# Retention and MLP on one core: a ring of ten turned chunks, one operation per state sum, step waits on the unit ahead, and new places for turns and steps

## The chip, the cores and the metric

The kernel runs on one core of a Trainium2 chip. The metric is device time in microseconds (us) of one execution, the median of several runs. A core has TensorE (PE, matmuls; its weight loads are shown as PEld), VectorE (DVE), ScalarE (ACT), GpSimd (POOL) and SyncE (SP), each with a queue that runs in order, and DMA engines that all queues share.

## The reference

Eight heads of causal retention (attention without softmax, with a decay per head) over eight sequences of 576 tokens, then an MLP with a sigmoid GELU over all 4608 tokens:

```python
scores = scale * np.matmul(q, k.transpose(0, 1, 3, 2))          # q, k, v: 8 x 8 x 576 x 64
gamma = 1.0 - 2.0 ** (-5.0 - np.arange(H, dtype=np.float32))
Dmat = np.where(rel >= 0, gamma[:, None, None] ** rel[None, :, :], 0.0)
attn_out = np.matmul(scores * Dmat[None, :, :, :], v)
x = attn_out.transpose(0, 2, 1, 3).reshape(B * S, H * D)         # 4608 x 512
h = x @ w_in                                                     # w_in: 512 x 2048
out = (h * (1.0 / (1.0 + np.exp(-1.702 * h)))) @ w_out           # w_out: 2048 x 512
```

## The kernel before, in words

**MLP.** The 4608 tokens are nine chunks of 512. For a chunk c, `hidden(c, f)` (L670) makes 128 hidden columns: four matmuls of 512 columns into a PSUM bank (psH[0], psH[1], and psU where it rotates over three), then a GELU on ACT that frees the bank. `hidden_half` (L705) does two f for half a chunk, eight matmuls of 256 columns. `project(c, r, g)` (L727) adds four of sixteen f for the row block r of 128 tokens; after g = 3 the bank is copied to one of three buffers osb (by DVE, or by ACT in chunk 0) and stored by SP. Each of these is a unit of four large matmuls (or eight half ones). From chunk 3 on, `region(c)` mixes the sixteen hidden units of chunk c with the sixteen projections of chunk c - 1, which all use psU.

**Retention.** A batch is five chunks of up to 128 tokens (chunk number n = 5 b + c) or nine blocks of 64. The decay is split into factors on v (`scale_v`, L344, on DVE) and on the output (gq); so a block needs masked scores within the block and a state, the running sum of k-transposed times v, across blocks. Batch 0 is done by chunks; batches 1 to 7 in 21 steps of three blocks, m = 0 to 20. `burst(m_out, m_in)` (L524) runs on PE some 90 matmuls of 64 x 64 x 64 back to back: values and state parts of the outputs of step m_out, and states and scores of step m_in = m_out + 1. Behind it DVE evacuates m_out to xT (`evac_wide`, which the MLP reads), masks the scores of m_in (`mask_wide`), adds the states up over the blocks into zacc (`state_wide`, L637) and casts them to zw, which the next burst reads. The state parts lie in columns 384 to 511 of PSUM banks 1 to 3 and in bank 4 (`z_at`, L520), which the transposes on PE also use.

**Loads and turns.** POOL's queue loads q, k and v chunk by chunk with a cast to bf16 into a ring of three batches; `step(m)` (L866) issues the loads of batch b + 3 into the freed places. The scores need q and k turned (head dimension on partitions). `turn(n)` does it on PE with a copy by ACT (chunks 4 to 9), `turn_dma(n)` (L481) with two DMA transposes on SP's queue, into a ring `qk` of NQK = 6 buffers; `step(m)` issues them six chunks ahead, so a turn waits until the slot's old chunk has been read. Stores of the output are on SP's queue too.

**The order.** It is written out by hand: `run(units, between)` (L880) calls the units in turn, and `between` names what is put behind unit i: turns, scalings, bursts, steps. `Rec` (L43) records each operation with what it reads and writes, derives the waits on semaphores, and leaves out a wait that an earlier one on the same queue covers. An operation's waits stand right before its first instruction, so what a burst needs is waited for inside the burst, part by part.

Of the kernel before, what the change touches and what calls it, by code (L numbers as in the profile page):

```python
# [27 lines left out]
NQK = 6  # L28
# [103 lines left out]
def bass_retnet_parallel__then__act_gelu_quick_kernel(  # L132
# [11 lines left out]
    with es:  # L144
# [373 lines left out]
        z_low = {0: (1, 384), 1: (3, 384), 2: (2, 384)}  # L518

        def z_at(blk, r):  # L520
            return z_low[blk] if r else (4, 128 * blk)


        def burst(m_out, m_in):  # L524
# [32 lines left out]
            def state(e, blk, first=()):  # L557
                g = blocks(m_in)[blk]
                for t in range(2):
                    for j in range(2):  # L560
                        for u in range(2):
                            h = 4 * u + 2 * t + j
                            bank, off = z_at(blk, place(g, u)[1])
# [6 lines left out]
            def score(e):  # L570
                for blk, g in enumerate(blocks(m_in)):
                    for t in range(2):
                        for u in range(2):
# [3 lines left out]
                            for j in range(2):  # L577
# [3 lines left out]
                                             start=(x == 0 and j == 0), stop=True,  # L581
# [12 lines left out]
            if m_in is not None:  # L594
                b, cs = chunks(m_in)
                rs = [(nm, b % NST, c) for nm in "kv" for c in cs]
                rq = [("qk", (NC * b + c) % NQK, 1) for c in cs] + queries(m_in)

                def state_a(e):
                    state(e, 1, (3, 4) if fresh else (4,))  # L600
                    return state(e, 0, (1,))
                before = R.op("PE", state_a, r=rs, ps=["S", "Z", "W"])
                R.op("PE", score, r=rq, ps=["S"])
                if m_in % 3 < 2:
                    R.op("PE", lambda e: state(e, 2, (2,) if fresh else ()), r=rs,
                         ps=["O", "W"], own=None if fresh else before)
                    done = None
                else:
                    done = done and before
# [6 lines left out]
            if m_in is not None:  # L616
                mask_wide(m_in)
                state_wide(m_in)
# [18 lines left out]
        def state_wide(m):  # L637
            keys = ["S", "W", "Z", "O"]

            def add(src, blk, lo, hi, first):  # L640
                to, was = zacc[:, blk, lo:hi], zacc[:, (blk - 1) % 3, lo:hi]
                if hi - lo == 256:
                    to, was = (x.rearrange("p (u x) -> p u x", u=2) for x in (to, was))
                if first:
                    R.op("DVE", lambda e: e.tensor_copy(to, src), w=[("zacc", blk)], ps=keys)
                else:
                    R.op("DVE", lambda e: e.tensor_tensor(to, was, src, ALU.add),  # L647
                         r=[("zacc", (blk - 1) % 3)], w=[("zacc", blk)], ps=keys)

# [347 lines left out]
```

## Time and profile before

| | |
|---|---|
| median of 3 runs | 319.37 us (316.39 to 320.68) |
| profiled execution | 318.88 us, of which 316.6 us are the span from the first to the last instruction |
| mean granted clock of TensorE over the span | 0.984 of full |
| DMA packets | 154848, of which 145472 under 512 bytes |

How to read it: the page gives busy shares of each engine and a picture of the span in 40 slices of 7.9 us. A row of the waits names the engine, the tile and line of the operation that waited, what released it, and the sum, the number and the longest of the waits in us. A row of the timeline gives start and length in us, engine, line, operation, output and inputs with shapes, how many, and in brackets the idle time before it with what ended it. A row of windows gives a stretch, then busy time of PE, PEld, DVE, ACT and POOL, the granted clock, the DMA share and GB/s. Ends of matmuls are modelled, and a few of their records are missing.

### The profile page before, as it was taken

To read this page: it belongs to the slowest core of one execution; us is meant where nothing else is said; L and a number is where in the kernel's file an instruction comes from. 1 tells how busy PE (TensorE), PEld (TensorE's weight loads), DVE (VectorE), ACT (ScalarE), POOL (GpSimd) and SP (SyncE) were. 2 spreads that over 40 slices of the span, in tenths; PEclk is the share of its full clock that TensorE was granted. 3 is DMA by queue.
4 is the path that set the end of the run, shared out by engine and by line. 5 is a ranking of instruction groups with operands and counts; after the bars stand their busy time and mean duration, and the time that the engine had idled before them with its cause. 6 is when DMAs were issued, how large, how long until landed. Compare 5 with 4: busy or idle time off the path is not lost.

```text
span 316.6 us, 7664 instructions
## 1 busy us (share of the span) xinstructions
PE 292.9 (93%) x3358; PEld 149.1 (47%) x3395; DVE 148.8 (47%) x274; ACT 108.3 (34%) x182; POOL 155.5 (49%) x208
## 2 busy tenths in 40 slices
PE   7799995979977977999999999999999999999996
PEld 3454443856733433444444444444444444444444
DVE  6699716066583775663462066606660420011011
ACT  8676240621403441333333332333233333333300
POOL 8999999999999999999610000000000000000000
PEclk9999998799997999999999999999999999999999
DMA  9999999999999999999999134313300000000102
GB/s 74 152 194 193 176 164 222 157 154 119 159 157 173 168 133 148 146 190 144 188 160 148 68 58 88 97 55 68 93 35 33 35 35 33 33 33 35 66 35 98
DMA packets 154848, 35.76 MB, mean 113 GB/s; under 512 B 145472, under 2 KB 150336, under 8 KB 154816
## 3 DMA queue, kind: packets, MB, share of 16 engines
q0 software_dynamic: 118384, 18.36, 83.3%
q1 hardware_dynamic: 36432, 16.92, 27.7%
q8 instruction: 26, 0.43, 0.5%
q14 instruction: 6, 0.05, 0.1%
HBM read 36.70 MB, written 9.44 MB: 146 GB/s over the span
## 4 chain that ended last, share of the span: by engine, by line
PE 76%; DVE 11%; DMA 5%; POOL 4%; issue 3%; POOLq 0%
PE psU L730 28%; PE psH L677 27%; PE psH L730 6%; DMA w_out_sb<-in_moe_w_out_dram 4%; PE psH L714 3%; DVE zacc L647 3%; PE psA L536 2%; PE psA L578 2%; DVE sm L634 2%; DVE xT L623 2%; PE psU L714 2%; DMA st_k<-in_k_dram 2%; PE psA L564 1%; POOL st_q L208 1%; PE psA L552 1%
## 5 line engine op out<-in xcount | busy, mean ns | idle before, releaser
L682 ACT ACTIVATE gT<-psH 128x512 bf16<-128x512 f32 x116 | 69.3, 597 | 147.4 <-PE psH L677 147.4
L677 PE MATMUL psH<-xT,w_in_sb 128*128 128x512 bf16 x453 | 110.3, 383 | 3.7 <-DVE osb L742 2.1
L730 PE MATMUL psU<-w_out_sb,gT 128*128 128x512 bf16 x416 | 100.9, 379 | 2.3 <-issue 2.2
L221 POOL DMA_DIRECT2D st_k<-in_k_dram x70 | 75.3, 1425 | 1.0 <-DVE st_v L291 1.0
L221 POOL DMA_DIRECT2D st_v<-in_v_dram x70 | 73.7, 1382 | 2.5 <-PE psA L552 2.5
L677 PEld LDWEIGHTS psH<-xT,w_in_sb 128*128 128x128 bf16 x464 | 43.5, 98 | 60.2 <-ACT gT L682 7.3
L730 PEld LDWEIGHTS psU<-w_out_sb,gT 128*128 128x128 bf16 x432 | 41.1, 98 | 47.8
L208 POOL DMA_DIRECT2D st_q<-in_q_dram x40 | 58.1, 1453 | 0.2 <-issue 0.2
L742 DVE COPY osb<-psU 128x512 f32<-128x512 f32 x26 | 17.9, 688 | 72.4 <-PE psU L730 72.4
L623 DVE TENSOR_TENSOR xT<-psA,gq 128x768 bf16<-128x768 f32 x21 | 20.1, 958 | 52.9 <-PE psA L552 52.9
L730 PE MATMUL psH<-w_out_sb,gT 128*128 128x512 bf16 x120 | 28.7, 379 | 1.4 <-issue 0.8
L634 DVE TENSOR_TENSOR sm<-psA,maskw 128x768 bf16<-128x768 f32 x21 | 19.9, 949 | 16.7 <-PE psA L564 16.7
L647 DVE TENSOR_TENSOR zacc<-zacc,psA 128x128 f32<-128x128 f32 (+1 forms) x77 | 24.8, 322 | 2.2
L350 DVE TENSOR_TENSOR st_v<-st_v,vfac 128x512 bf16<-128x512 bf16 x37 | 24.2, 681 | 3.4 <-DMA st_v<-in_v_dram 3.4
L730 PEld LDWEIGHTS psH<-w_out_sb,gT 128*128 128x128 bf16 x128 | 11.9, 98 | 14.0 <-DMA w_out_sb<-in_moe_w_out_dram 0.9
L536 PE MATMUL psA<-sm,st_v 64*64 64x64 bf16 x504 | 11.9, 197 | 3.0 <-DVE zw L663 2.8
L371 ACT ACTIVATE qk<-psA 128x1024 bf16<-128x1024 bf16 x10 | 10.2, 1023 | 11.7 <-PE psA L365 11.7
L714 PE MATMUL psH<-xT,w_in_sb 128*128 128x256 bf16 x88 | 12.8, 298 | 1.1 <-DVE xT L623 1.1
L536 PEld LDWEIGHTS psA<-sm,st_v 64*64 64x64 bf16 x504 | 7.6, 107 | 12.4 <-issue 6.8
L720 ACT ACTIVATE gT<-psH 128x512 bf16<-128x512 f32 x11 | 6.6, 598 | 18.7 <-PE psH L714 18.7
L663 DVE CAST zw<-zacc 128x768 bf16<-128x768 f32 (+1 forms) x21 | 11.6, 550 | 0.7
L564 PE MATMUL psA<-st_v,st_k 64*64 64x64 bf16 x448 | 9.9, 195 | 1.4 <-DVE st_v L350 1.4
(99 smaller groups left out, 199.9 us busy)
## 6 DMA issues: line engine op xcount, KB each, us to landing
out_dram<-osb SPq DMA_DIRECT2D x35, 256.0 KB, 2.0
st_q<-in_q_dram POOLq DMA_DIRECT2D x32, 128.0 KB, 11.3
st_k<-in_k_dram POOLq DMA_DIRECT2D x57, 64.0 KB, 11.6
st_v<-in_v_dram POOLq DMA_DIRECT2D x57, 64.0 KB, 12.2
w_out_sb<-in_moe_w_out_dram POOLq DMA_DIRECT2D x4, 512.0 KB, 11.1
w_in_sb<-in_moe_w_in_dram POOLq DMA_DIRECT2D x3, 512.0 KB, 8.4
st_k<-in_k_dram POOLq DMA_DIRECT2D x4, 128.0 KB, 4.2
st_v<-in_v_dram POOLq DMA_DIRECT2D x4, 128.0 KB, 4.8
```

The source lines that it names most:

```text
L208: R.op("POOL", lambda e, d=d, s=s: e.dma_start(d, s), w=[(nm, sl, c)], dma=(nm, sl, c))
L221: R.op("POOL", lambda e: [e.dma_start(d, s) for d, s in parts], w=[(nm, sl, c)], dma=(nm, sl, c), parts=2)
L350: R.op(eng, lambda e: e.tensor_tensor(t, t, f, ALU.mult), r=[("vfac", min(b, 1))], w=[("v", sl, c)])
L536: i = e.matmul(psA[half(t), 2 + u, at : at + 64], rows_of(st_v, m_out, g, u, 4 * u + 2 * t + j), smw[si(m_out)][half(r), j, 2 * blk + t, : ...
L623: R.op("DVE", lambda e: e.tensor_tensor(xT[:, :, t0 : t0 + 192].rearrange("p (u j) n -> p u j n", u=2), psA[:, 2:4, 0:384].rearrange("p u ...
L634: R.op("DVE", lambda e: e.tensor_tensor(o, i, k, ALU.mult), r=["maskw"], w=[("sm", si(m))], ps=["S"])
L647: R.op("DVE", lambda e: e.tensor_tensor(to, was, src, ALU.add), r=[("zacc", (blk - 1) % 3)], w=[("zacc", blk)], ps=keys)
L677: i = e.matmul(bank.ap(), w_in_sb[:, a, 128 * f : 128 * f + 128], xT[:, a, 512 * c : 512 * c + 512], start=(a == 0), stop=(a == 3))
L682: R.op("ACT", lambda e: e.activation(gT[c % 2][:, f, :], bank.ap(), AF.Gelu_apprx_sigmoid), w=[("gT", c % 2, f)], ps=[key])
L714: m = e.matmul(bank[:, 256 * i : 256 * i + 256], w_in_sb[:, a, 128 * (f + i) : 128 * (f + i) + 128], xT[:, a, a0 : a0 + 256], start=(a == ...
L730: i = e.matmul(bank, gT[c % 2][:, f, 128 * r : 128 * r + 128], w_out_sb[:, f, :], start=(f == 0), stop=(f == NF - 1))
L742: R.op("DVE", lambda e: e.tensor_copy(osb[m].ap(), bank), w=[("osb", m)], ps=[key])
```

## The change

- `NQK` 6 to 10: ten buffers for turned chunks. `step(m)` now issues the turns of the chunks of step m + 5 (`turn_step`), before its loads; steps 3 and 4 are turned ahead of step 0.
- `z_at` is keyed by step, block and half u in place of the row half r, so that the two parts of one state always lie as one access pattern with two segments: `state_wide` adds each block with one operation of 2 x 128 columns; it took two of 128 for each block of odd number.
- PE's order within a burst: state of block 1, scores, then the states of blocks 0 and 2 as one operation.
- `needs(m_out, m_in)` lists all that a burst reads. `run` gives that list as `ahead` to the unit in front of a `step`, which waits for it before its first matmul. Bursts that aren't in a `step`, and `hidden_half`, don't do so.
- The first burst comes one unit earlier, adds its states before the mask and has them cast by ACT.
- Step 2 also takes in step 3 (its states and scores were a burst of their own, four half units into the second half of chunk 1). Other places move by a unit or so; chunk 2's hidden units begin on psH[1] in place of psH[0].

The diff, cut to its core:

```diff
-NQK = 6
+NQK = 10
...
-        z_low = {0: (1, 384), 1: (3, 384), 2: (2, 384)}
-
-        def z_at(blk, r):
-            return z_low[blk] if r else (4, 128 * blk)
-
-
-        def burst(m_out, m_in):
+        def z_at(m, blk, u):
+            if u == 0:
+                return 4, 128 * blk
+            odd = blocks(m)[blk] % 2
+            return (3 if odd else 2) if blk == 2 else 1 - odd, 384
+
+
+        def needs(m_out, m_in):
+            r = []
+            if m_out is not None:
+                b, cs = chunks(m_out)
+                r += [("sm", si(m_out)), "zw"] + [("v", b % NST, c) for c in cs] + queries(m_out)
+            if m_in is not None:
+                b, cs = chunks(m_in)
+                r += [(nm, b % NST, c) for nm in "kv" for c in cs]
+                r += [("qk", (NC * b + c) % NQK, 1) for c in cs] + queries(m_in)
+            return r
+
+        def burst(m_out, m_in, cast="DVE"):
...
-                    state(e, 1, (3, 4) if fresh else (4,))
-                    return state(e, 0, (1,))
-                before = R.op("PE", state_a, r=rs, ps=["S", "Z", "W"])
-                R.op("PE", score, r=rq, ps=["S"])
-                if m_in % 3 < 2:
-                    R.op("PE", lambda e: state(e, 2, (2,) if fresh else ()), r=rs,
-                         ps=["O", "W"], own=None if fresh else before)
-                    done = None
-                else:
-                    done = done and before
+                opened = z_at(m_in, 1, 1)[0]
+                done = R.op("PE", lambda e: state(e, 1, (opened, 4)), r=rs, ps=["S", "W"])
+                R.op("PE", lambda e: score(e, (1 - opened,)), r=rq, ps=["S"])
+
+                def state_b(e):
+                    i = state(e, 0)
+                    if m_in % 3 < 2:
+                        i = state(e, 2, (2, 3) if fresh else ())
...
                 R.op("PE", phase_y, r=ro, ps=["O", "Z"], own=done)
                 evac_wide(m_out)
-            if m_in is not None:
+            if m_in is not None and cast == "ACT":
+                state_wide(m_in, cast)
                 mask_wide(m_in)
-                state_wide(m_in)
+            elif m_in is not None:
+                mask_wide(m_in)
...
-        def state_wide(m):
-            keys = ["S", "W", "Z", "O"]
-
-            def add(src, blk, lo, hi, first):
-                to, was = zacc[:, blk, lo:hi], zacc[:, (blk - 1) % 3, lo:hi]
-                if hi - lo == 256:
-                    to, was = (x.rearrange("p (u x) -> p u x", u=2) for x in (to, was))
-                if first:
-                    R.op("DVE", lambda e: e.tensor_copy(to, src), w=[("zacc", blk)], ps=keys)
-                else:
-                    R.op("DVE", lambda e: e.tensor_tensor(to, was, src, ALU.add),
-                         r=[("zacc", (blk - 1) % 3)], w=[("zacc", blk)], ps=keys)
-
+        def state_wide(m, cast):
             flat = psA.ap().rearrange("p a n -> p (a n)")
             gs = [g for g in blocks(m) if g < NBLK - 1]
             for blk, g in enumerate(gs):
-                (b1, o1), (b0, o0) = z_at(blk, 1), z_at(blk, 0)
-                at1, at0 = 512 * b1 + o1, 512 * b0 + o0
-                if g % 2 == 0:
-                    src = flat[:, at1 : at1 + 128]
-                    src = bass.AP(src.tensor, src.offset, [src.ap[0], [at0 - at1, 2], [1, 128]])
-                    add(src, blk, 0, 256, g == 0)
+                at1, at0 = (512 * x + y for x, y in (z_at(m, blk, 1), z_at(m, blk, 0)))
+                src = flat[:, at1 : at1 + 128]
+                src = bass.AP(src.tensor, src.offset, [src.ap[0], [at0 - at1, 2], [1, 128]])
+                to, was = (zacc[:, x % 3, :].rearrange("p (u x) -> p u x", u=2)
+                           for x in (blk, blk - 1))
+                if g == 0:
+                    R.op("DVE", lambda e, to=to, src=src: e.tensor_copy(to, src),
+                         w=[("zacc", blk)], ps=["S", "W", "Z", "O"])
                 else:
-                    add(flat[:, at0 : at0 + 128], blk, 0, 128, False)
-                    add(flat[:, at1 : at1 + 128], blk, 128, 256, False)
+                    R.op("DVE", lambda e, to=to, src=src, was=was: e.tensor_tensor(
+                        to, was, src, ALU.add),
+                        r=[("zacc", (blk - 1) % 3)], w=[("zacc", blk)], ps=["S", "W", "Z", "O"])
             z = zw[:, gs[0] + 1 : gs[0] + 1 + len(gs)].rearrange("p b u t d -> p b (u t d)")
-            R.op("DVE", lambda e: e.tensor_copy(z, zacc[:, 0 : len(gs), :]),
-                 r=[("zacc", x) for x in range(len(gs))], w=["zw"])
+            r = [("zacc", x) for x in range(len(gs))]
+            if cast == "ACT":
+                R.op("ACT", lambda e: e.activation(z, zacc[:, 0 : len(gs), :], AF.Copy), r=r, w=["zw"])
+            else:
+                R.op("DVE", lambda e: e.tensor_copy(z, zacc[:, 0 : len(gs), :]), r=r, w=["zw"])
...
+        def hidden(c, f, rotate=2, ahead=()):
...
+            R.op("PE", fn, r=[("w_in", f // 2)] + [("xT", x) for x in toks] + list(ahead), ps=[key])
...
         def step(m, into=True):
             b, i = 1 + m // 3, m % 3
             burst(m, m + 1 if into and m + 1 < NWIDE else None)
+            turn_step(m + 5)
             for c in ((0,), (1, 2), (3, 4))[i]:
-                n = NC * b + c + NQK
-                if PE_TURNS <= n < NSTEP:
-                    turn_dma(n)
                 if b + NST < B:
                     load(b + NST, c)
+        def step_chunks(m):
+            return [NC * (1 + m // 3) + c for c in ((0, 1), (2, 3), (4,))[m % 3]] if m < NWIDE else []
+
+        def turn_step(m):
+            for n in step_chunks(m):
+                turn_dma(n)
+
         def scale(m):
-            for c in ((0, 1), (2, 3), (4,))[m % 3]:
-                scale_v(NC * (1 + m // 3) + c)
+            for n in step_chunks(m):
+                scale_v(n)
         def run(units, between):
             for i, unit in enumerate(units):
-                unit()
+                ahead = []
+                for fn, *args in between.get(i, ()):
+                    if fn is step:
+                        ahead += needs(args[0], args[0] + 1 if len(args) < 2
+                                       and args[0] + 1 < NWIDE else None)
+                unit(ahead)
                 for fn, *args in between.get(i, ()):
                     fn(*args)
         def unit_h(c, half, f):
-            return lambda: hidden_half(c, half, f)
+            return lambda ahead: hidden_half(c, half, f)
         def unit_o(c, r, g, bank, eng="DVE"):
-            return lambda: project(c, r, g, *bank, eng=eng)
+            return lambda ahead: project(c, r, g, *bank, eng=eng, ahead=ahead)
         run([unit_o(0, r, g, wide_banks[(1, 2, 0)[r]], "ACT") for g in range(4) for r in range(3)]
             + [unit_o(0, 3, g, wide_banks[1], "ACT") for g in range(4)],
             {1: [(tail_turn,)], 3: [(intra, 4)], 5: [(tail_out,)], 6: [(turn, 5)],
-             8: [(scale_v, 5)], 12: [(turn, 6), (scale_v, 6)], 14: [(burst, None, 0)]})
+             8: [(scale_v, 5)], 11: [(turn, 6), (scale_v, 6)], 13: [(burst, None, 0, "ACT")]})
+        turn_step(3)
+        turn_step(4)
         step(0, False)
-        turn_dma(10)
         hcount[0] = 16
         run([unit_h(1, 0, f) for f in range(0, NF, 2)],
             {0: [(turn, 7), (scale_v, 7)], 2: [(turn, 8), (scale_v, 8)],
-             5: [(burst, None, 1)], 6: [(turn, 9), (scale_v, 9)]})
+             4: [(turn, 9), (scale_v, 9)], 6: [(burst, None, 1)]})
         run([unit_o(1, r, g, wide_banks[(1, 2)[r]]) for r in range(2) for g in range(4)],
-            {0: [(step, 1)], 4: [(step, 2, False)], 5: [(scale, 3)]})
+            {0: [(scale, 3)], 1: [(step, 1)], 5: [(step, 2)]})
         run([unit_h(1, 1, f) for f in range(0, NF, 2)],
-            {3: [(burst, None, 3)], 5: [(scale, 4)]})
+            {3: [(scale, 4)]})
         run([unit_o(1, r, g, wide_banks[(0, 1)[r - 2]]) for r in range(2, 4) for g in range(4)],
-            {1: [(step, 3)], 3: [(scale, 5)], 5: [(step, 4)]})
-        hcount[0] = 0
-        run([lambda f=f: hidden(2, f, 3) for f in range(NF)],
-            {1: [(scale, 6)], 3: [(step, 5)], 5: [(scale, 7)], 8: [(step, 6)],
-             10: [(scale, 8)], 13: [(step, 7)]})
+            {0: [(step, 3)], 2: [(scale, 5)], 4: [(step, 4)]})
+        hcount[0] = 1
+        run([lambda ahead, f=f: hidden(2, f, 3, ahead) for f in range(NF)],
+            {0: [(scale, 6)], 2: [(step, 5)], 5: [(scale, 7)], 7: [(step, 6)],
+             10: [(scale, 8)], 12: [(step, 7)]})
```

20 lines of the change are left out of this document (10 added, 10 removed).

## The prediction

> **What bounds the kernel now.** I read the page first, for the shares and the slices of the span.
>
> ```profile
> span 316.6 us, 7664 instructions
> ...
> PE 292.9 (93%) x3358; PEld 149.1 (47%) x3395; DVE 148.8 (47%) x274; ACT 108.3 (34%) x182; POOL 155.5 (49%) x208
> ...
> PE   7799995979977977999999999999999999999996
> ...
> DMA  9999999999999999999999134313300000000102
> ```
>
> TensorE is the bound, but its slices show two halves: from the sixteenth slice on it is full, and between slices 6 and 16 (about 42 to 125 us) it is not, while the DMA engines are. Nearly all that placing can win lies in that stretch. Next the waits of PE, in total us, times and longest:
>
> ```profile
> PE psA L536 <- DVE zw L663: 2.8, 2, 2.2
> PE psA L578 <- issue: 2.5, 2, 1.8
> PE psH L677 <- DVE osb L742: 2.1, 1, 2.1
> PE psA L365 <- DVE zacc L647: 1.6, 1, 1.6
> PE psA L564 <- DVE st_v L350: 1.4, 3, 0.8
> ...
> PE psH L714 <- DVE xT L623: 1.1, 1, 1.1
> ...
> PE psH L677 <- DVE zacc L647: 0.8, 1, 0.8
> ```
>
> Except for the second row they are all waits for VectorE, and none is for a turned chunk: the ring of six cost TensorE nothing here. The 0.8 is region 3's first hidden unit on bank psH[0], which the last unit of chunk 2 (15 mod 3 = 0) used just before; ACT's GELU is what it waits for, whatever the label says. Third the stretches by window, for the granted clock (the number behind those of the five engines, 1.00 being full):
>
> ```profile
> 93.78:97.19 3.41, 1.27 (x7) 0.42 (x6) 3.31 (x8) 0.00 (x0) 3.41 (x6) 1.00 1.79 142
> 97.19:100.60 3.41, 3.41 (x10) 1.22 (x9) 0.86 (x2) 0.90 (x2) 3.41 (x7) 0.50 1.64 186
> 121.08:124.49 3.41, 1.48 (x44) 0.94 (x38) 1.08 (x2) 0.00 (x0) 3.41 (x6) 1.00 1.74 138
> ```
> ```profile
> 53.78:62.85 9.07, 9.07 (x64) 7.06 (x64) 1.14 (x2) 4.82 (x7) 9.07 (x14) 0.68 2.12 167
> ```
>
> After a stretch of 3.41 us with 1.27 us of PE work the clock is halved (0.50 in the next row); a stretch with 1.48 did not halve it. So the two long waits cost twice: behind the 2.2 us one 9.07 x (1 - 0.68) = 2.9 us, behind the 2.1 us one 3.41 x 0.50 = 1.7 us. Together 4.6 us.
>
> **The pieces for the sum.** PE first, then VectorE behind a step (one step of the steady half), then the forms.
>
> ```profile
> 126.91 2.59 PE psH L677 x12
> ```
> ```profile
> 198.00 1.03 PE L730 MATMUL psU<-w_out_sb,gT 128*128 128x512 bf16 x4
> 198.96 0.32 PE L536 MATMUL psA<-sm,st_v 64*64 64x64 bf16 x16
> 199.11 0.23 PE L552 MATMUL psA<-qk,zw 64*64 64x64 bf16 x8
> ...
> 200.10 0.81 PE L730 MATMUL psU<-w_out_sb,gT 128*128 128x512 bf16 x3 [0.16 <-issue]
> ```
> ```profile
> 192.09 0.96 DVE L623 TENSOR_TENSOR xT<-psA,gq 128x768 bf16<-128x768 f32 x1 [2.66 <-PE psA L552]
> 192.96 0.94 DVE L634 TENSOR_TENSOR sm<-psA,maskw 128x768 bf16<-128x768 f32 x1
> 193.82 0.41 DVE L645 COPY zacc<-psA 128x256 f32<-128x256 f32 x1
> 194.27 1.06 DVE L647 TENSOR_TENSOR zacc<-zacc,psA 128x128 f32<-128x128 f32 x3
> 195.37 0.56 DVE L663 CAST zw<-zacc 128x768 bf16<-128x768 f32 x1
> 195.84 0.68 DVE L742 COPY osb<-psU 128x512 f32<-128x512 f32 x1
> 196.45 1.28 DVE L350 TENSOR_TENSOR st_v<-st_v,vfac 128x512 bf16<-128x512 bf16 x2
> ```
> ```profile
> L647 DVE TENSOR_TENSOR zacc<-zacc,psA 128x128 f32<-128x128 f32 x56 | 16.0, 286 | 1.7
> ...
> L647 DVE TENSOR_TENSOR zacc<-zacc,psA 128x256 f32<-128x256 f32 x21 | 8.8, 417 | 0.5
> L663 DVE CAST zw<-zacc 128x512 bf16<-128x512 f32 x7 | 3.0, 429 | 0.2
> ```
>
> A matmul of 512 columns takes 2.59 / 12 = 0.216 us, a unit of four 0.86. A full step takes about 1.0 us: from 198.96 to 200.10, less 0.216, since of the next unit only three of four records are there. So the unit behind this step began at about 199.88.
>
> *State sums.* A block of two 128-column parts took two operations of 286 ns when its number is odd and one of 417 ns when even; now always one. Four blocks of eight in each batch change: 4 x (572 - 417) = 0.6 us of VectorE per batch, 28 operations less in all. VectorE is 47% busy, so this counts only where its chain ends a wait. The bounds for the new operation are 417 (same pattern of two parts) and 572; I take 417, which starts every 0.45 us.
> The chain behind a step, counted from the start of the next unit: evacuation begins at 0.12, takes 0.87, mask 0.87, three sums 1.35, cast 0.56: 3.77 us; with two sums and the short cast, when a batch ends, 0.12 + 0.87 + 0.87 + 0.90 + 0.43 = 3.19. An output copy adds 0.61, a scaling of one chunk 0.65, of two 1.28.
>
> *Waits on the unit ahead.* The unit before a step now waits for all that the step needs. What stands behind it on PE is the whole program, so the cover of VectorE's chain is one unit (0.86) shorter at each step. In the regions from chunk 3 on, seven units remain: 7 x 0.86 = 6.04 against 3.77 + 0.61 + 1.28 = 5.66 us. No wait there, by 0.4 us. In the crowded stretch the cover is shorter, and each place has a new wait (chain, then cover):
> - step 1: behind a burst without outputs there is no evacuation: 3.77 - 0.87 = 2.9, plus 0.05 to reach PE, less 2 units: 1.2
> - step 2: 3.19 + 0.05 - 3 units = 0.65
> - second unit of the second half of chunk 1, on psH[1]: step 2 now carries the next batch's scores and sums, and row block 1's output copy queues behind them: 3.77 + 0.68 + 0.05 - 3 units = 1.9
> - step 4: 3.77 + 0.65 + 0.05 - 3 units = 1.9
> - step 5: 3.19 + 0.68 + 1.28 + 0.05 - 5 units = 0.9
> - step 6: 3.77 + 1.28 + 0.05 - 4 units = 1.65
> - step 7: 3.77 + 0.65 + 0.05 - 4 units = 1.0
> - step 8: 3.19 + 1.28 + 0.05 - 4 units = 1.1
>
> What the waits give back is at the steps themselves. The first small matmul came 0.31 us after the last large one (198.00 + 3 x 0.216 to 198.96), 0.095 more than the cadence; and where the scores of a new batch wait for turned chunks there is a hole:
>
> ```profile
> 102.39 0.30 PE L564 MATMUL psA<-st_v,st_k 64*64 64x64 bf16 x16
> 102.68 0.38 PE L578 MATMUL psA<-qk 64*64 64x64 bf16 x24
> ```
>
> Sixteen take 0.15 (198.96 to 199.11), so 0.14 us is lost there, at seven of some twenty steps. Per step the gain is between 0 and 0.095 + 0.14 = 0.23; I take 0.11, as the lead may belong to the change of tile shape: 20 x 0.11 = 2.2 us. The waits themselves, once met, are taken at nothing ahead of a unit, since 0.86 us of large matmuls of the unit before run meanwhile; were that cover gone, 0.14 each would come back.
>
> *First burst.* It moves one unit ahead (two units now cover it, not one), its sums go before the mask, and its cast to ACT. ACT's price is not in the trace for this form; the nearest rows are
>
> ```profile
> L682 ACT ACTIVATE gT<-psH 128x512 bf16<-128x512 f32 x116 | 69.3, 597 | 147.4 <-PE psH L677 147.4
> ...
> L371 ACT ACTIVATE qk<-psA 128x1024 bf16<-128x1024 bf16 x10 | 10.2, 1023 | 11.7 <-PE psA L365 11.7
> ```
>
> so 0.60 to 1.02, midway 0.81, beside the mask's 0.95 and hidden by it (if ACT took more than 0.95, the rest would lie on the path). Chain: 0.12 + 1.35 + 0.95 + 0.05 = 2.47, less 1.73 = 0.75, in place of 2.2. The 1.1 for xT behind it stays. Idle there falls to 0.75 + 1.0, so 1.65 us of a 3.41 us stretch is work, above the 1.48 that kept the clock: I count the 2.9 us as gone.
> *Turn 9 before burst 1*: the 1.6 for the bank of the turns goes; late next is step 1, above. *Bank order of chunk 2* (starts on psH[1]): the 2.1, its 1.7 of half clock and the 0.8 go; late next are steps 5 and 8. *Step 2 merged with burst 3*: one restart of about 0.2 less.
> *Ring of ten.* Turns no longer wait for a free slot but for the loads:
>
> ```profile
> SPq L484 <- PE psA L552: 29.3, 12, 6.8
> ```
> ```profile
> 93.50 2.22 POOL L221 DMA_DIRECT2D st_k<-in_k_dram  x2
> ```
> ```profile
> st_k<-in_k_dram POOLq DMA_DIRECT2D x2, 64.0 KB, 13.2
> qk<-st_q SPq DMA_TRANSPOSE x1, 7.3
> ```
>
> Direct gain 0, as TensorE never waited for them. They pass the output stores on SP: each store now stands behind the turns of five steps ahead, and those behind their loads. The tightest is chunk 23 (its load of k is the row at 93.50): it lands at about 107.5 (94.2 for its second half + 13.2), and is ready at about 117, 2 us of SP's queue and 7.3 from issue later. Step 8 ended at about 123.3 (row 122.90 below); 7 us earlier, and with seven units behind it, step 9 wants chunk 23 at about 122. POOL's own queue keeps its order.
>
> **The sum**, against the profiled execution (318.88 us, span 316.6), which is 0.15% under the median of the runs, 319.37. Gone or replaced: the waits 2.8 + 2.1 + 1.6 + 1.4 + 0.8 = 8.7. They are eight, and each is about 0.18 longer from start to start than the profile's idle, which counts from the modelled end of a matmul (sixteen show 0.32 where 0.15 pass): + 1.4 = 10.1. Clock 4.6, merged burst 0.2, and the mid-operation stalls 2.5 + 0.36 = 2.9. Total 17.8. New: 0.75 + 1.2 + 0.65 + 1.9 + 1.9 + 0.9 + 1.65 + 1.0 + 1.1 = 11.05, and half of the mid-operation stalls, 1.45 (below): 12.5. 17.8 - 12.5 + 2.2 = 7.5; from this I take 0.6 for loads that the earlier turns delay (the late-turns rival below costs 3 and I count a fifth of it): 6.9. Time 318.9 - 6.9 = 312.0.
>
> The mid-operation stalls fall inside one operation, where no wait can be, beside one instruction packet (DMA view of 119 to 120.5 us):
>
> ```profile
> 122.90 0.22 PE L578 MATMUL psA<-qk 64*64 64x64 bf16 x4 [1.77 <-issue]
> ```
> ```profile
> q8 instruction: 1, 0.02, 4.9%
> ```
>
> The bounds after the change are 0 and 2.9, since where a block of instructions ends moves: half. [...]
>
> **Rivals.**
> - *The new waits halve the clock.* Two are 1.9 us and leave 3.41 - 1.9 = 1.51 us of work in a stretch, the line lies between 1.27 and 1.48; step 0's place is as near. One such costs 1.7, two 3.4: 313.7 to 315.4. For: nearness, and stretches can begin elsewhere. Against: each alone lies on the good side. [...]
> - *Turns late.* Two or three more chunks are turned by 110 us than before, on full DMA engines. If chunk 23 comes 7 us later, step 9 waits 2 us, and a store behind the turns can hold an output copy for 1 more: 315.
> - *Slower.* The shorter cover fails in the regions: if the chain takes 7.2 us in place of 5.66 (two-part sums at 572, copies waiting for stores), each of twelve steps waits 1.2: 14 us, 326. It decides from 0.6 a step (chain 6.6) on. Against it: the steady rows above end at 197.73, 5.85 behind their unit, before the saving.
> - *No stalls in mid-operation, step gain at 0.2*: 309.
>
> **How the numbers follow.** Chances: forecast 0.53 (310.5 to 313.5), last rival 0.12, half clock 0.15, late turns 0.12, slower 0.08. The range 308.5 to 316.5 holds all but the last and the tails. About 2% (6.4 us, 313.0 from the median) is what a measurement here can tell from no change: faster 0.60 (most of the forecast and the last rival), same 0.32, slower 0.08.
>
> **What would show it.** Right: clock 1.00 from 50 to 100 us; a wait of about 1.9 before the second unit of the second half of chunk 1, labelled osb; PE waits on zw or st_v now before large units (L730, L677) instead of L536 and L564; no hole ahead of the scores; step 0's wait under 1 us. Wrong: waits on turned chunks or on stores, a half clock behind the 1.9 us waits, or waits before the regions' steps.

## The result and the profile after

The changed kernel takes 315.25 us (median of 18 runs, 313.65 to 316.96) against 318.12 (18 runs, 316.39 to 320.68) beside it: a ratio of 0.9901, interval 0.9872 to 0.9929. The gain is clear of the noise, about 2.9 us, and under the 2% line. The profiled execution took 316.69 us (span 314.8); that of before 318.88 (316.6).

The page's span, busy shares, PE's slices, the granted clock and the DMA slices of the kernel after:

```profile
span 314.8 us, 7671 instructions
...
PE 296.1 (94%) x3395; PEld 148.7 (47%) x3395; DVE 144.2 (46%) x245; ACT 109.0 (35%) x183; POOL 155.0 (49%) x208
...
PE   7899987977979788999999999999999999999996
...
PEclk9999999899899999999999999999999999999999
DMA  9999999999999999999999995100000000000112
```

The picture is the old one: a stretch up to about 125 us in which TensorE is not full, then full slices. The DMA engines are full far beyond it, to about 189 us here (24 slices of 7.87 us) and 174 us before. Two slices still show a lowered clock. The waits of PE (total us, times, longest):

```profile
PE psH L722 <- DVE osb L750: 2.0, 1, 2.0
...
PE psU L685 <- DVE st_v L350: 1.7, 1, 1.7
PE psH L738 <- DVE st_v L350: 1.7, 1, 1.7
PE psH L738 <- DVE zw L672: 1.6, 2, 1.1
PE psH L685 <- DVE st_v L350: 1.4, 2, 0.9
...
PE psH L722 <- DVE xT L637: 1.1, 1, 1.1
PE psH L738 <- DMA w_out_sb<-in_moe_w_out_dram: 0.8, 1, 0.8
PE psU L738 <- DVE st_v L350: 0.7, 1, 0.7
PE psA L576 <- issue: 0.7, 1, 0.7
PE psA L548 <- ACT zw L670: 0.6, 1, 0.6
```

As the prediction said, the waits now stand ahead of large units (L685, L738, L722) and no longer inside bursts, apart from step 0's (the last row). They are not shorter: the waits for VectorE and ScalarE shown here sum to 10.8 us; those of the prediction's list, from before, sum to 9.8. The stretches around the two places with a lowered clock (us, busy time of PE, PEld, DVE, ACT and POOL, granted clock, DMA share, GB/s):

```profile
50.20:53.61 3.41, 1.68 (x51) 1.37 (x51) 2.42 (x4) 1.07 (x2) 3.41 (x6) 1.00 1.81 238
53.61:57.02 3.41, 3.41 (x22) 2.66 (x21) 0.80 (x2) 2.22 (x3) 3.41 (x5) 0.50 2.10 198
74.09:77.50 3.41, 1.40 (x12) 0.92 (x11) 3.31 (x7) 0.60 (x1) 3.41 (x6) 1.00 2.53 137
77.50:80.92 3.42, 3.42 (x18) 2.44 (x17) 0.99 (x2) 0.65 (x2) 3.42 (x7) 0.50 1.37 121
```

In this execution the clock is halved behind step 0's two short waits, and again behind the 2.0 us wait for the output copy: half of 3.41 us, 1.7, at each place.

One profile says little about the clock here, though. Each run lists its mean granted clock, and it comes in steps of about 0.0054 (0.995, 0.989, 0.984 and 0.978 in the runs), which is one stretch of 3.41 us at half clock (3.41 x 0.5 / 315). Of 69 runs of the kernel before, taken beside the experiments, none had full clock throughout; their mean is 0.9896, or 1.9 such stretches. 26 runs with one stretch have a median of 316.9 us, 25 with two 317.8, 16 with three 318.5 (the other two have four): about 0.8 us a stretch. Of the 18 runs of the kernel after, 12 had full clock (median 314.5), four one stretch (316.0), two had two (316.8, the profiled one among them): mean 0.9976, or 0.44 stretches. So about 1.5 stretches fewer at 0.8 to 1.2 us each, 1.2 to 1.8 us of the 2.9, are clock. This is an estimate from differences between runs; the clock alone does not tell the time of a variant, as experiments 2 and 9 show.

### The profile page after: what moved, and what is told of

Same layout as the page of the kernel before. It is cut to its first block, busy times and chain, and to the rows that moved or that the text cites. A ratio compares the mean times of both kernels' runs of the same rounds, so it can differ in the third digit from the quotient of the medians.

```text
span 314.8 us, 7671 instructions
## 1 busy us (share of the span) xinstructions
PE 296.1 (94%) x3395; PEld 148.7 (47%) x3395; DVE 144.2 (46%) x245; ACT 109.0 (35%) x183; POOL 155.0 (49%) x208
## 4 chain that ended last, share of the span: by engine, by line
PE 77%; DVE 14%; DMA 4%; POOL 2%; issue 2%; ACT 1%; POOLq 0%
PE psU L738 28%; PE psH L685 27%; PE psH L738 4%; DMA w_out_sb<-in_moe_w_out_dram 4%; PE psH L722 3%; DVE zacc L664 3%; DVE xT L637 2%; PE psA L548 2%; DVE sm L648 2%; PE psH L799 2%; PE psA L576 2%; PE psU L722 2%; DVE st_v L350 2%; PE psA L365 1%; PE psA L590 1%
## 5 line engine op out<-in xcount | busy, mean ns | idle before, releaser
L685 PE MATMUL psH<-xT,w_in_sb 128*128 128x512 bf16 x464 | 110.2, 379 | 1.4 <-DVE st_v L350 1.4
L738 PE MATMUL psU<-w_out_sb,gT 128*128 128x512 bf16 x432 | 104.5, 379 | 0.7 <-DVE st_v L350 0.7
L685 PEld LDWEIGHTS psH<-xT,w_in_sb 128*128 128x128 bf16 x464 | 43.1, 98 | 58.1 <-ACT gT L690 7.3
L221 POOL DMA_DIRECT2D st_k<-in_k_dram x70 | 65.6, 1140 | 4.6 <-issue 3.6
L221 POOL DMA_DIRECT2D st_v<-in_v_dram x70 | 65.1, 1139 | 0.0
L738 PEld LDWEIGHTS psU<-w_out_sb,gT 128*128 128x128 bf16 x432 | 41.0, 98 | 48.8 <-DVE st_v L350 1.4
L208 POOL DMA_DIRECT2D st_q<-in_q_dram x40 | 48.4, 1209 | 5.8 <-issue 5.8
L738 PE MATMUL psH<-w_out_sb,gT 128*128 128x512 bf16 x128 | 30.3, 380 | 4.1 <-DVE st_v L350 1.7
L664 DVE TENSOR_TENSOR zacc<-zacc,psA 128x256 f32<-128x256 f32 x49 | 20.5, 418 | 1.2
L738 PEld LDWEIGHTS psH<-w_out_sb,gT 128*128 128x128 bf16 x128 | 11.6, 98 | 18.4 <-DVE zw L672 2.6
L722 PE MATMUL psH<-xT,w_in_sb 128*128 128x256 bf16 x88 | 12.3, 294 | 3.1 <-DVE osb L750 2.0
L576 PE MATMUL psA<-st_v,st_k 64*64 64x64 bf16 x448 | 11.6, 197 | 0.7 <-issue 0.7
L685 PE MATMUL psU<-xT,w_in_sb 128*128 128x512 bf16 x40 | 10.3, 380 | 1.8 <-DVE st_v L350 1.7
```

Of the source, the lines that this page charges most:

```text
L208: R.op("POOL", lambda e, d=d, s=s: e.dma_start(d, s), w=[(nm, sl, c)], dma=(nm, sl, c))
L221: R.op("POOL", lambda e: [e.dma_start(d, s) for d, s in parts], w=[(nm, sl, c)], dma=(nm, sl, c), parts=2)
L664: R.op("DVE", lambda e, to=to, src=src, was=was: e.tensor_tensor(to, was, src, ALU.add), r=[("zacc", (blk - 1) % 3)], w=[("zacc", blk)], p ...
L685: i = e.matmul(bank.ap(), w_in_sb[:, a, 128 * f : 128 * f + 128], xT[:, a, 512 * c : 512 * c + 512], start=(a == 0), stop=(a == 3))
L722: m = e.matmul(bank[:, 256 * i : 256 * i + 256], w_in_sb[:, a, 128 * (f + i) : 128 * (f + i) + 128], xT[:, a, a0 : a0 + 256], start=(a == ...
L738: i = e.matmul(bank, gT[c % 2][:, f, 128 * r : 128 * r + 128], w_out_sb[:, f, :], start=(f == 0), stop=(f == NF - 1))
```

## The experiments

Ratios are to the kernel before, run beside them (317.73, 317.67 and 318.17 us in the three groups); that of the kernel after is 0.9901.

**1. Without the attached waits.** In the changed kernel:

```
-                unit(ahead)
+                unit(())
```

> The changed kernel with the waits back inside the burst (nothing is waited for on the unit ahead). Theory A, the moved places carry the gain and the waits on the unit ahead cost one unit of cover each: the waits of the changed trace before steps 1, 2, 4, 5, 6, 7 and 8 (1.3, 0.5, 1.9, 0.7, 1.9, 1.0, 1.0 us) lose up to 0.86 each, 5.6 us in all, so about 310 us, ratio to the kernel before about 0.974. Theory B, the waits on the unit ahead carry the gain by closing holes at some twenty steps: 2 to 4 us are lost, 317 to 319 us, ratio 0.997 or more.

Measured: 313.95 us (6 runs), 0.9877, interval 0.9838 to 0.9915. Neither theory's number: without the waits the ratio is 0.24% (0.8 us) lower, well inside the intervals. The profile shows one reason why so little moves; below its row are two rows of the DMA view of 107 to 110.6 us, the busy share in 40 slices of 0.09 us and the instruction queue:

```profile
110.53 0.31 PE L590 MATMUL psA<-qk 64*64 64x64 bf16 x5 [2.50 <-issue]
```
```profile
DMA  9999999999999999991111011115999999999999
q8 instruction: 1, 0.02, 1.9%
```

It is a stop of 2.5 us in the middle of one operation, where no semaphore can be. The view has one packet of 16384 bytes of instructions, which begins at 107.55 us. In the midst of the stop, from 108.6 to 109.4 us, the DMA engines are nearly idle. In the changed kernel the one such stop is 0.7 us. (Followed up in 8, 11 and 12.)

**2. Ring of six again**, turns issued six chunks ahead, in the changed kernel:

```
-NQK = 10
+NQK = 6
...
-            turn_step(m + 5)
             for c in ((0,), (1, 2), (3, 4))[i]:
+                n = NC * b + c + NQK
+                if PE_TURNS <= n < NSTEP:
+                    turn_dma(n)
```

> The changed kernel with the ring of six and turns six chunks ahead, as before. Theory A, the ring costs and gives nothing on TensorE, since no trace shows a wait for a turned chunk: 315 us, within 0.5 us of the changed kernel, and no wait of PE on a turn. Theory B, the ring is what lets the steps come earlier: waits of PE at the scores or before the units, 317 us or more.

Measured: 317.69 us (12 runs), 1.0006, interval 0.9984 to 1.0029. The whole gain is gone, and one row names the reason:

```profile
106.46 0.81 PE L685 MATMUL psU<-xT,w_in_sb 128*128 128x512 bf16 x3 [3.18 <-DMA qk<-st_k]
```

TensorE never waited for a turned chunk before; with earlier steps and waits attached to the unit ahead it does. The clock did not go back: five of the 12 runs have full clock, and their mean is 0.996, as with the first burst alone (6).

**3. Bank order alone**, in the kernel before: `hcount[0] = 1` ahead of chunk 2.

> The kernel before with one number changed: chunk 2's hidden units begin on psH[1]. Theory A, the wait of 2.1 us for the output copy, the half clock of 3.4 us behind it (1.7 us) and the 0.8 us at region 3 go: 318.1 - 4.8 = 313.3 us if nothing takes their place, ratio 0.985; at least 2.3 us. Theory B, the next waits for VectorE take up what it frees: under 1 us, ratio above 0.997.

Measured: 317.11 us (12 runs), 0.998, interval 0.9948 to 1.0012: nothing measurable. The 2.1 us wait for the copy became 0.4, but the next waits grew, zw from 2.8 (2) and st_v from 1.4 (3):

```profile
PE psA L536 <- DVE zw L663: 3.2, 3, 2.2
PE psA L578 <- issue: 2.5, 2, 1.3
PE psA L564 <- DVE st_v L350: 2.4, 4, 0.8
```

**4. The burst and one-operation sums alone**: the changed kernel's burst and sums, with ring, issue and places of before and no attached waits.

> The changed burst and one operation per state sum, in the places of before, with the ring of six and no wait on the unit ahead. Theory A: VectorE's chain is 0.2 to 0.4 us shorter at the six places where PE waits for it, and each step some hundredths: 1.5 us less, 316.6 us, ratio 0.995. Theory B, the sums and the new order of the burst carry most of the gain: 315.5 us or less, ratio 0.992 or below.

Measured: 318.24 us (12 runs), 1.001, interval 0.9981 to 1.0039. Theory A's 0.995 lies outside the interval: the sums and the burst's new order are worth nothing measurable in the old places.

**5. Row block 1's output copy on ScalarE**, in the changed kernel:

```
-        run([unit_o(1, r, g, wide_banks[(1, 2)[r]]) for r in range(2) for g in range(4)],
+        run([unit_o(1, r, g, wide_banks[(1, 2)[r]], ("DVE", "ACT")[r]) for r in range(2) for g in range(4)],
```

> The kernel after the change, with one edit: the output copies of row block 1 of chunk 1 go to ScalarE and not to VectorE, so that the second unit of that chunk's second half no longer waits 2.02 us for a copy that stands behind a step's sums. In the kernel after the change this wait is followed by 3.41 us at half clock, a loss of 1.7. Theory A (the wait and the half clock behind it are lost time, and nothing else stands ready to take their place): 2.0 and 1.7 go, and 0.3 to 1.0 us comes back as ScalarE's own work in the places after it, so 2.7 to 3.4 us less than the kernel after the change, a ratio of about 0.980 to the kernel before, and a mean clock of 0.995. Theory B (a wait that goes comes back at the next place, as it did where one bank was rotated in the kernel before): ratio 0.988 to 0.992, and the waits of the steps 3 and 4 grow by what the copy's wait loses.

Measured: 312.86 us (6 runs, 312.57 to 313.58), 0.9866, interval 0.9833 to 0.9899. Between the two theories and nearer to B; 0.35% under the changed kernel's ratio, with overlapping intervals. The 2.0 us wait and its half clock are gone, and a part came back: st_v ahead of L685 went from 1.7 and 1.4 to 2.0 and 2.1, zw from 1.6 to 2.4:

```profile
PE psH L738 <- DVE zw L672: 2.4, 2, 1.9
PE psH L685 <- DVE st_v L350: 2.1, 2, 1.3
PE psU L685 <- DVE st_v L350: 2.0, 1, 2.0
```

**6. The first burst alone**, in the kernel before (the cast's argument is carried down to the state sums as in the change):

```
-             8: [(scale_v, 5)], 12: [(turn, 6), (scale_v, 6)], 14: [(burst, None, 0)]})
+             8: [(scale_v, 5)], 11: [(turn, 6), (scale_v, 6)], 13: [(burst, None, 0, "ACT")]})
```

> The kernel before the change with the first burst alone changed: recorded one place earlier, its turn and scaling one place earlier too, its sums ahead of its mask, and the cast to bf16 on ScalarE. In the pair of profiles step 0 began 1.1 us earlier after the change, with a wait of 0.75 in place of 2.8 us. Theory A (this part is worth its own wait): 1.0 to 2.1 us less than the kernel before, ratio 0.993 to 0.997, and the wait of step 0 at 0.6 to 0.8 us. Theory B (the steps behind it are bound by turns and sums of their own, and take it up): ratio 0.998 or more, with a later wait longer by about 1 us.

Measured: 315.45 us (12 runs), 0.9925, interval 0.9896 to 0.9954: a little more than theory A's best, and nearly the gain of the whole change. The wait is as long as forecast, the second row here:

```profile
PE psH L683 <- DVE osb L748: 2.1, 1, 2.1
...
PE psA L536 <- ACT zw L668: 0.8, 1, 0.8
```

And the mean clock of its runs is 0.996, with five of 12 at full clock, against 0.990 and none. In the profile step 0 begins at 51.87 us, hardly ahead of the 51.92 of before, mainly because w_out's load came later in this execution. First the kernel before, then this one:

```profile
42.46 1.90 PE L730 MATMUL psH<-w_out_sb,gT 128*128 128x512 bf16 x8 [0.45 <-DMA w_out_sb<-in_moe_w_out_dram]
51.92 0.32 PE L536 MATMUL psA<-sm,st_v 64*64 64x64 bf16 x16 [2.19 <-DVE zw L663]
```
```profile
43.82 1.90 PE L736 MATMUL psH<-w_out_sb,gT 128*128 128x512 bf16 x8 [1.05 <-DMA w_out_sb<-in_moe_w_out_dram]
51.87 0.32 PE L536 MATMUL psA<-sm,st_v 64*64 64x64 bf16 x16 [0.77 <-ACT zw L668]
```

From the unit that waits for the load to step 0 it is 9.46 us before and 8.05 here, so the wait itself gives back 1.4 us, and the clock comes on top. The edit's parts (the place, the order of sums and mask, ScalarE's cast) were not run one by one.

**7. The reverse: the first burst as before, all else changed.**

```
-             8: [(scale_v, 5)], 11: [(turn, 6), (scale_v, 6)], 13: [(burst, None, 0, "ACT")]})
+             8: [(scale_v, 5)], 12: [(turn, 6), (scale_v, 6)], 14: [(burst, None, 0)]})
```

> The kernel after the change with its first burst set back to what it was before: one unit later, its turn one unit later, its mask ahead of its sums and its cast on VectorE. In the kernel before, the same edit made the other way was worth 2.4 us (ratio 0.9925, interval 0.9896 to 0.9954), and the mean granted clock of its executions rose from 0.990 to 0.996. Theory A (the first burst carries nearly the whole gain, in either surroundings): about 317.6 us, a ratio of 0.997 to 1.002, a wait of 2 us or more at step 0 and a mean granted clock of 0.992 or less. Theory B (ring, places and attached waits carry their own share, and the first burst's wait only moves to later places): ratio 0.993 or less.

Measured: 318.01 us (12 runs), 1.0029, interval 0.9997 to 1.0061; none of the 12 at full clock, mean 0.990. Theory A. Step 0 and the stretches around it (us, PE busy, clock, DMA share, GB/s):

```profile
52.83 0.32 PE L548 MATMUL psA<-sm,st_v 64*64 64x64 bf16 x16 [2.35 <-DVE zw L672]
```
```profile
50.35:53.76 3.41, 0.82 (x41) 1.00 1.78 241
53.76:57.17 3.41, 2.49 (x16) 0.50 2.20 187
57.17:60.58 3.41, 3.41 (x19) 0.50 2.33 158
```

The 2.35 us wait leaves 0.82 us of work in a stretch, and two stretches at half clock follow (the profile is of the slowest of the 12 runs, 321.42 us). Ring, places, sums and attached waits together, without the first burst, win nothing. The profiles of all kernels here agree on the clock: behind step 0 it is halved in all four with the old first burst, and in five of ten with the new one.

**8. Copy on ScalarE and earlier scalings**, in the changed kernel with attached waits. Each scaling from step 4's on is recorded ahead of the step that it stood behind, as here:

```
-            {0: [(scale, 3)], 1: [(step, 1)], 5: [(step, 2)]})
+            {0: [(scale, 3)], 1: [(step, 1)], 4: [(scale, 4)], 5: [(step, 2)]})
...
-            {3: [(scale, 4)]})
+            {6: [(scale, 5)]})
```

> As the run with the copy on ScalarE, and each scaling of a chunk's values from step 4 on is recorded before the step ahead of it and not behind it, so that VectorE has it done when the units with the attached waits ask for it. In the kernel after the change the waits for scaled values are 1.7, 1.7, 1.4 (two) and 0.7 us, 5.5 in all. Theory A (VectorE's order is what the waits hang on): 3 to 4.5 us of the 5.5 go, since what is asked for next, the state's bf16 copy, was done 0.5 to 1 us ahead of the scalings; ratio 0.968 to 0.973. Theory B (the state's own chain is as late as the scalings, so that the same waits stand there under the name of the state or of the masked scores): within 0.3% of the run with the copy alone.

Measured: 314.11 us (6 runs), 0.989, interval 0.9841 to 0.9939. Theory B's number, and a part of its reason. Of the waits for scaled values only 0.2 us is left in the profile. The waits for zw rose from 1.6 us in the changed kernel to 4.0 (3.1, 0.6 and 0.3), as theory B says; and stops inside operations rose from 0.7 to 3.8 us, which neither theory has. The profiled run (311.87 us) is one of the two fastest of the six, so how far the profile stands for the median is open:

```profile
PE psH L738 <- DVE zw L672: 3.1, 3, 1.4
PE psA L576 <- issue: 2.1, 2, 1.2
```
```profile
101.98 0.24 PE L576 MATMUL psA<-st_v,st_k 64*64 64x64 bf16 x5 [0.93 <-issue]
109.44 0.25 PE L590 MATMUL psA<-qk 64*64 64x64 bf16 x7 [0.98 <-issue]
116.48 0.29 PE L576 MATMUL psA<-st_v,st_k 64*64 64x64 bf16 x13 [1.16 <-issue]
```

The trace's instruction packets of this stretch begin at 99.64, 106.84 and 114.10, each 1.2 to 1.6 us ahead of the stop.

**9. Ring of six without attached waits**: the edits of 1 and 2 together.

> The kernel after the change with both the ring of six (turns issued six chunks ahead, behind the step that frees the place) and no wait attached to the MLP unit. With the waits attached the ring of six lost the whole gain (ratio 1.0006, one unit waiting 3.2 us for a turned chunk); without them, but with the ring of ten, the ratio was 0.9877. Theory A (the ring matters only because the attached waits ask for the turn one unit, 1.73 us, earlier): the 3.2 us wait shrinks to 1.5 or less, ratio 0.988 to 0.993. Theory B (the ring is needed by the earlier places of the steps alone): a wait for a turned chunk of 2 us or more stays, ratio 0.997 to 1.002.

Measured: 315.48 us (12 runs), 0.9937, interval 0.9908 to 0.9967, just beside theory A's range. No wait for a turned chunk is left, so that wait does come from the attached waits. (A unit is 0.86 us; the 1.73 of the expectation is two.) Against 1 (0.9877) the ring of ten looks worth 0.6% even here; the intervals just touch, and what would carry it shows only as longer stops (2.5 and 1.2 us inside L590) and more half clock (mean 0.989). That stays open. This kernel has none of its 12 runs at full clock, like the kernel before, and is still 0.6% faster than that one: what it wins does not show as clock.

**10. First burst and bank order**, in the kernel before: the edits of 6 and 3 and nothing else.

> The kernel before the change with two small edits: the changed first burst, and chunk 2 starting on the second MLP bank. The first alone gave 0.9925; the second alone gave 0.998 (interval 0.9948 to 1.0012), since the next waits for VectorE took what the 2.1 us wait for an output copy had cost. Theory A (with the first half clock gone, the second wait is worth its 2.1 us and the half clock behind it): 2 to 3.5 us less than with the first burst alone, ratio 0.982 to 0.986. Theory B (the wait moves to the next places as before): ratio 0.990 to 0.9935.

Measured: 313.16 us (6 runs), 0.9863, interval 0.9819 to 0.9907. Theory A's direction, a little under its size. Two small edits do what the whole change does (0.9901), or a little more; the intervals overlap. The 2.1 us wait is now

```profile
PE psH L683 <- DVE osb L748: 0.4, 1, 0.4
```

and three of six runs have full clock, where edit 3 alone had none of 12.

**11. Copy on ScalarE without attached waits**: the edits of 1 and 5.

> The kernel after the change with ScalarE's copy for row block 1 (0.9866 alone) and no wait attached to the MLP units (0.9877 alone, against 0.9901 for the kernel after the change). Theory A (attached waits and stalls in the middle of a burst stand for each other: where TensorE does not wait ahead of a unit, it stops inside the burst for its next 16384 bytes of instructions, 2.5 us in one place without the attached waits against 0.7 with them): within 0.25% of the copy alone, 0.984 to 0.989, with stalls of 2 to 4 us inside bursts. Theory B (the two edits add): ratio 0.982 to 0.9845.

Measured: 313.43 us (6 runs), 0.9862, interval 0.982 to 0.9905. Theory A, though the interval reaches into theory B's range: no sign that the two add, and stops by issue of 2.3 (two), 1.4 and 1.4 us stand inside the bursts. That TensorE stops there for its instructions is the theory's assumption; no run shows what it waits for.

**12. All three**: the edits of 1, 5 and 8.

> As the run before this one (copy on ScalarE, no attached waits), with the scalings recorded a step earlier too. With attached waits the earlier scalings took 5.5 us of waits for scaled values out of the profile and made no difference in time (0.989 against 0.9866, intervals overlapping), while stalls inside bursts rose from 0.7 to 3.8 us. Theory A (what is left in the stretch from 95 to 125 us is the supply of instructions to TensorE beside full DMA engines, not VectorE): within 0.3% of the run without the earlier scalings. Theory B (VectorE's chain ends the waits): 1.5 us or more less than that run, ratio 0.980 or less.

Measured: 312.85 us (6 runs), 0.9846, interval 0.9804 to 0.9888; theory A's number, within 0.2% of 11, with 3.9 us of stops in L576, whose cause is not shown here either. This has the lowest ratio, but 5, 10, 11 and 12 can't be told apart. All four lie 0.35 to 0.55% under the changed kernel's ratio, with overlapping intervals, and 1.3 to 1.5% under the kernel before.

## Why the prediction was right, and where it was wrong

The range held (308.5 to 316.5) and the direction was right. The size was not: 2.9 us were won where the sum has 6.9, the likeliest value, 312.0, was 3.2 us too low, and the time stayed within 2% of before, for which the chance was 0.32 against 0.60 for faster. The range held because it was wide enough for the rivals. Rival 1, the half clock behind the new waits, came true in the profiled execution with both its places: its 313.7 to 315.4 holds the measured time. But that is in part luck: in 12 of 18 runs neither place was halved, and even these, at 314.5, are 2.5 us over the forecast. By the sum's own terms, in the profiled pair:

- *Half clock, 4.6 gone: the largest miss.* The stretch at step 0 was sized rightly, 1.65 us of work forecast and 1.68 there. The line was wrong: 1.48 had kept the clock in another place, and 1.68 did not here. The second place, 1.51 forecast and 1.40 there, was halved too. 3.4 us came back. Over all runs the clock did about half of the work (1.2 to 1.8 of 2.9 us) where the sum has two thirds, and from a smaller loss: the profile of before had three half-clock stretches where the mean of its runs is 1.9, and a stretch costs about 0.8 us and not 1.7, since part of it is given back in waits that end later anyway. This last is argued; the 0.8 is a difference between runs.
- *Step gain, 2.2: failed where it can be read.* The first steady burst and the last one begin, before and after:

```profile
130.29 0.32 PE L536 MATMUL psA<-sm,st_v 64*64 64x64 bf16 x16
...
252.54 0.32 PE L536 MATMUL psA<-sm,st_v 64*64 64x64 bf16 x16
```
```profile
128.71 0.32 PE L548 MATMUL psA<-sm,st_v 64*64 64x64 bf16 x16
...
250.79 0.32 PE L548 MATMUL psA<-sm,st_v 64*64 64x64 bf16 x16
```

  122.25 us became 122.08: 0.17 over eleven steps, 0.015 each in place of 0.11. The lead to the first small matmul is 0.31 as before, so it did not come from waits inside the burst. That it belongs to the change of tile shape, the prediction's lower bound, fits this and was not tried by itself.
- *New waits, 11.05: right.* Idle ahead of the units: step 0 0.58 (0.75 forecast), step 1 1.1 (1.2), step 2 0.5 (0.65), the copy 2.0 (1.9), step 4 1.7 (1.9), step 5 0.6 (0.9), step 6 1.7 (1.65), step 7 0.9 (1.0), step 8 0.75 (1.1): 9.8, and 11.4 with the 0.18 that each adds from start to start. That the covers of units and the VectorE chains can be counted so well is the part to copy. Their two prices were good too:

```profile
L664 DVE TENSOR_TENSOR zacc<-zacc,psA 128x256 f32<-128x256 f32 x49 | 20.5, 418 | 1.2
...
L670 ACT ACTIVATE zw<-zacc 128x768 bf16<-128x768 f32 x1 | 0.8, 843 | 2.6 <-DVE zacc L664 2.6
```

  418 ns for 417 taken, 0.84 us for 0.81.
- *Stops inside an operation, 1.45 of 2.9 left: right in direction.* 0.7 is left in the list of waits, 0.9 with its 0.18. That a stop hangs on where a block of instructions ends, from which the sum took its half, no run shows: of the nine packets of 16384 bytes that begin between 45 and 125 us, two are followed by a stop in the profile of before and one in that of after. What the forecast did not see is that stops grow where waits go: from 0.7 us in the changed kernel to 2.5 (1), 3.8 (8), 5.1 (11) and, in L576 alone, 3.9 (12). Attached waits do not rule them out: experiment 7, which has them, shows stops of 1.6 and 0.9.
- *Ring of ten, direct gain 0: right for the old places only.* Under the attached waits a ring of six costs the whole gain (2). The prediction looked at who waits now, and not at who would wait once all else was earlier.
- *Late loads, 0.6, and stores behind turns*: nothing of them in the waits. In their place the wait for w_out's load ahead of step 0 is 0.4 us longer, unforecast; it is 0.3 to 1.0 us over the profiles of all kernels here, so this is scatter.

Taken together, -3.4 (clock) - 2.0 (step gain) - 0.4 (waits) - 0.4 (w_out) + 0.6 (late loads) + 0.5 (stops) = -5.1, against the 4.7 by which the profiled pair's gain (2.2) missed 6.9.

The slower rival did not come: in the regions from chunk 3 on only the unit ahead of step 8 waits, 0.75 us, which the sum had listed. And the gain needs one part above all: with the first burst alone the kernel has 0.9925, with all but it 1.0029. Given the attached waits it needs the ring of ten too, as with a ring of six nothing is left (1.0006).

## What to carry to other kernels

The wait to shorten first was here the one that left TensorE 1.03 us of work in a clock stretch of 3.41: one burst moved by one unit, with its cast on another engine, was worth nearly the whole change (0.9925 against 0.9901). Read the clock from many runs and not from one profile, since the kernel before fell on one to four stretches at half clock from run to run. And before a resource is called free because nobody waits for it, ask again with everything ahead of it done sooner (3.2 us for a turned chunk in experiment 2). Waits that went came back in part, at the next place on the same chain or as stops inside an operation: in experiment 8 zw rose from 1.6 to 4.0 us and the stops from 0.7 to 3.8.

## What the runs showed of the hardware

In every trace with changes of the clock they lie on a grid of 3.413 us: from the first record of the clock on, 47.787, 6.827, 37.547 and 3.413 us apart before (14, 2, 11 and 1 times 3.413), and 47.787, 3.413, 20.480 and 3.413 after (14, 1, 6 and 1). The grid's start differs from one execution to the next: the first record of the clock, at full, lay 2.87, 3.22, 4.01 and 5.02 us behind TensorE's first matmul in four traces (experiment 6, before, after, experiment 10). That this is why the kernel after has full clock in 12 of its 18 runs and not in the other six is inferred and not shown. Single waits of 2.02 us (after) and 2.35 us (experiment 7) were followed by half clock. In experiment 6 the 2.1 us wait that halved the clock in the kernel before was cut by an edge, with 1.84 us of idle left in the first row's stretch, and no half clock followed (same columns as above):

```profile
93.43:96.84 3.41, 1.57 (x8) 0.75 (x9) 2.87 (x7) 0.50 (x1) 3.41 (x7) 1.00 2.05 192
96.84:100.26 3.42, 3.42 (x108) 1.91 (x107) 0.23 (x1) 1.89 (x4) 3.42 (x7) 1.00 1.69 156
```

Over the traces whose grid can be read, take the stretches of 3.41 us with full clock that begin between 40 and 125 us. Every one with up to 1.47 us of PE work (thirteen) was followed by half clock, and none with 1.76 or more. Of the seventeen between, six were. No line in busy time parts these, and the number of matmul records does not either: 1.72 us of 68 records kept the clock in experiment 11, 1.71 us of 66 did not in experiment 2 (each with the stretch behind it; us, PE busy, clock, DMA share, GB/s):

```profile
98.20:101.61 3.41, 1.72 (x68) 1.00 1.93 158
101.61:105.02 3.41, 3.41 (x17) 1.00 1.54 199
```
```profile
111.91:115.33 3.42, 1.71 (x66) 1.00 2.04 136
115.33:118.74 3.41, 3.08 (x49) 0.50 2.27 148
```

What decides there stays open. The 1.48 that kept the clock before and the 1.68 that did not after both lie in this band, so the prediction's 1.65 stood on uncertain ground.

Instructions come in packets of 16384 bytes on queue q8: between 45 and 125 us they begin 6.6 to 11.5 us apart before and 7.2 to 10.3 after. The stops inside an operation there, 0.72 and 1.77 us before and 0.67 after, begin 2.0, 1.1 and 1.9 us behind the start of a packet; the longest in the profiles here is 2.7 us (experiment 4). In these two traces no stop comes later than 123 us. Full DMA engines alone do not make them: in the changed kernel the engines stay full to about 189 us, further packets come (at 133.97, 142.14 and 156.34 us), and no stop follows. In the 2.5 us stop of experiment 1 the engines were even nearly idle for 0.8 us. What TensorE waits for in a stop is not shown.
